# Batch 0's first three query blocks take seven second channel products from sums kept in the score squares' buffers

## The chip, the cores and the metric

One Trainium2 chip, one core. The metric is the device time of one execution in microseconds (us); a kernel's time is the median of its runs.

## The reference

Eight batches of a gated attention unit, followed by a mixer layer. With S = 3008, D = 256:

```
scores = z z^T / S                     (z: 3008 x 64, so scores are symmetric)
attn   = relu(scores)^2 @ v
x      = u * attn
h      = relu(x^T @ w_tok1) @ w_tok2   (token mixing, 256 wide)
u2     = x + h^T
out    = u2 + relu(u2 @ w_ch1) @ w_ch2 (channel mixing, 1536 wide)
```

## The kernel before, in words

A batch is cut into NQ = 6 query blocks of 512 rows (the last has 448) and, in the same places, into NG = 6 key groups of four 128-row tiles. A program of the host writes out the order of all instructions by hand: it keeps a modelled clock for TensorE (PE), ScalarE (ACT), VectorE (DVE) and the queue of SP, and at each step picks a unit of scores, half a group of attention (av), or a piece of the mixer. Its modelled times decide the order in which instructions are issued; on the chip, each engine works through its own list and waits only for data and buffers.

**Attention.** For block (b, q) and group g, two score units are made (L465), each of two 128 x 512 tiles, followed by a relu on ScalarE (L503; L491 for the half blocks on the diagonal, called triangles) and a square on VectorE (L511, L542). The squares lie in buffers of the tag `at`, of which there are six, 4 KB in each partition. As the scores are symmetric, a block's squares are also transposed by a DMA on SP's queue (`flip`, L562) into a buffer of the tag `fl` (eleven, also of 4 KB) and serve block (b, g) there; so in batch 1, block (1, q) scores only the groups g >= q, and (1, 3) scores three. Then v is multiplied in (L692), and two halves of the sum are added and gated by u (L820, L826, L846). `can_score` lets scores run ahead of the attention as long as `at` has room, and in batch 1 as far as one query block ahead.

**Mixing.** The mixer of batch b runs inside the attention of batch b + 1, in two stretches, in which no scores and no attention are issued: `goals` opens batch 0's token products at block (1, 2), its second token product and the channel mixing of its query blocks 0 to 2 (HALF = 3) at (1, 3), and the rest, with the first three blocks of batch 1, at (2, 0). Pieces of the mixer are:

- `tok1` (L1029) and `tok2` (L1086), with the addition of h to x on VectorE (L1095), and a transpose of u2 on SP (L1114);
- `ch1` (L1143): one of six parts of a query block's first channel product, four 128 x 512 matmuls into a pair of PSUM banks, evacuated with a relu to `h2pre` by ScalarE (L1182) or VectorE (L1184); the rule `on_act` chooses the engine from the modelled loads, and VectorE's limit is 1 us later for b > 0 than for batch 0;
- `ch2` (L1366): the second channel product by 128-row tiles, 12 matmuls of 128 x 256 for each of a block's four tiles, and `residual` (L1383), which adds u2 and sends the rows out;
- `product` (L1280): the second channel product in another form, used where `fast(q)` holds. The 2 x 2 blocks of (row tiles, channel tiles) are multiplied with seven products and not eight, in the manner of Strassen and Winograd. Each of the seven has 2 x 6 matmuls of 128 x 128 (half as many for the last query block). They take four sums of the hidden layer's tiles (`make_sums`, L1223, L1228, L1232, L1235, three times in a block, each into one `hsum` buffer), and sums of the weights (`mix_weights`, L989, made once). Each product is collected on VectorE with an addition into `ro` (L1317), and after the seventh `ro` is sent out. Product 5 waits for the addition of product 2, 6 for 1, 3 for 5, 7 for 6, 4 for 7, as they share banks.

In the kernel before, `fast(q)` holds for every query block but batch 0's first three and the very last one. `hsum` and `ro` lie in `fl`.

Around the second channel product of block q, parts of the first product of block q + 1 are issued early ("borrowed"): two in the ch2 form, five between the seven products. The sums of a borrowed query block 3 are put off (`late_sums`) to the last query block of the attention.

Of the kernel before, what the change touches and what calls it, by code (L numbers as in the profile page):

```python
# [57 lines left out]
def kernel(  # L58
# [914 lines left out]
    def mix_weights(t):  # L973
# [19 lines left out]

        step(t)

    VERY_LAST = (B - 1, NQ - 1, CHT // 2 - 1)
    ORDER_LAST = (1, 2, 6, 5, 0, 7, 3, 0, 4)

    def add_mixer(b):
# [130 lines left out]
        def ch1(q, c2, borrowed, end):  # L1130
            slots = [take_slot()[0] for _ in range(1 + ((b, q, c2) == VERY_LAST))]
            W = widths[q]
            xT = xTs[b, q]
            if c2 % 2 == 0:
                live["h2"] += 1
                st["h2", q, c2 // 2] = sb.tile(
                    [P, 4, QW], BF16, tag="h2", name="h2pre", bufs=ROOM["h2"])
            hps = [bank_pair(slot, "hp") for slot in slots]
            hp = hps[0]
            for r in range(2):  # L1140
                cc = 2 * c2 + r
                for dc in range(DT):
                    nc.tensor.matmul(  # L1143
                        hps[r % len(hps)][:, r, :W], w_ch1_sb[:, dc, cc * P:(cc + 1) * P],
                        xT[:, dc, :W], start=(dc == 0), stop=(dc == DT - 1))
            h2 = st["h2", q, c2 // 2][:, 2 * (c2 % 2):2 * (c2 % 2) + 2, :]

            def load(e):
                return max(free[e], end) + sum(op.busy for op in waiting[e])

            def keep_ends():
                if c2 == 0 and b % 2 == 0:
                    pair["hs"] = sb.tile([P, CHT, P], BF16, tag="hs", name="hs", bufs=1)
                r = b % 2 * TAIL
                copier = nc.gpsimd if b < B - 1 else nc.vector
                copier.tensor_copy(  # L1156
                    pair["hs"][:, 2 * c2:2 * c2 + 2, r:r + TAIL], h2[:, :, W - TAIL:W])

            if (b, q, c2) == VERY_LAST:
                landed, freed = [], Done()  # L1160

                def evacuate_part(r, t):
                    if r:
                        nc.scalar.activation(h2[:, r, :W], hps[1][:, r, :W], ACT.Relu)
                    else:
                        nc.vector.tensor_single_scalar(h2[:, r, :W], hp[:, r, :W], 0.0, AX.max)
                    landed.append(t)
                    if len(landed) == 2:
                        h2_done[q, c2].t = freed.t = max(landed)
                        keep_ends()  # L1170

                for r, engine, at, busy in ((0, "dve", end - 0.18, 0.62), (1, "act", end + 0.21, 0.5)):
                    push(engine, at, busy, busy + 0.16, lambda t, r=r: evacuate_part(r, t))
                ring.extend((freed, slot) for slot in slots)
                release("xT", xT_uses[q])
                return
            on_act = load("act") + 0.92 < load("dve") + 1.15 + (b > 0)

            def evacuate(t):
                recent[0] = h2[:, 0, :1]  # L1180
                if on_act:
                    nc.scalar.activation(h2[:, :, :W], hp[:, :, :W], ACT.Relu)  # L1182
                else:
                    nc.vector.tensor_single_scalar(h2[:, :, :W], hp[:, :, :W], 0.0, AX.max)  # L1184
                if q == NQ - 1:
                    keep_ends()
                if fast(q) and c2 % 2:
                    if borrowed and q == HALF and b < B - 1:
                        late_sums.append(lambda t: make_sums(q, c2 // 2, t))
                    else:  # L1190
                        make_sums(q, c2 // 2, t)
            engine, busy = ("act", 0.92) if on_act else ("dve", 1.15)
            ring.append((push(engine, end + 0.21, busy, busy + 0.16, evacuate,
                              done=h2_done[q, c2]), slots[0]))
            if c2 == CHT // 2 - 1:
                release("xT", xT_uses[q])
# [11 lines left out]
        def make_sums(q, d, t):  # L1208


            n = pairs_of(q)
            busy = 0.34 if n == 2 else 0.21
            sums = {}

            def kind(k):
                return sums["s"][:, k, :, :n, :]

            def add1(t):
                sums["s"] = sb.tile([P, 4, 2, 2, P], BF16, tag="fl", name="hsum", bufs=ROOM["fl"])
                st["sum", q, d] = sums["s"]  # L1220
                live["fl"] += 1
                fl_free.pop(0)
                nc.vector.tensor_add(kind(0), tiles_of(q, d, 0, 1), tiles_of(q, d, 1, 1))  # L1223
                push("dve", t - 0.05, busy, busy + 0.15, add3, done=s_done[q, d, 2])
                push("dve", t, busy, busy + 0.15, add2, done=s_done[q, d, 1])

            def add2(t):
                nc.vector.tensor_sub(kind(1), kind(0), tiles_of(q, d, 0, 0))  # L1228
                push("dve", t, busy, busy + 0.15, add4, done=s_done[q, d, 3])

            def add3(t):
                nc.vector.tensor_sub(kind(2), tiles_of(q, d, 0, 0), tiles_of(q, d, 0, 1))  # L1232

            def add4(t):
                nc.vector.tensor_sub(kind(3), tiles_of(q, d, 1, 0), kind(1))  # L1235

            push("dve", t, busy, busy + 0.15, add1, room=("fl",), frees=fl_free,
                 done=s_done[q, d, 0])

        h2_uses = [1] * NQ  # L1240
# [13 lines left out]
        def product(q, k, end):  # L1254
# [30 lines left out]
                done_with_h2(q)  # L1285
            if k == 7:
                for d in range(CHT // 4):
                    release("fl", [1], end + 0.2)
            collect(q, k, end)

        def collect(q, k, end):
# [17 lines left out]

            def add(t):  # L1310
                if k == 1:
                    st["res", q] = sb.tile([P, QW // P, D], F32, tag="fl", name="ro",
                                           bufs=ROOM["fl"])
                    live["fl"] += 1
                    fl_free.pop(0)
                m, h = blocks_of[k]
                nc.vector.tensor_add(  # L1317
                    res(m, h), source, us(m, h) if opening else res(m, h))
                recent[0] = st["res", q][:, 0, :1]
                over[q] -= 1  # L1320
                if not over[q]:
                    nc.sync.dma_start(
                        out=rows_of(out[b], q)[:, :2 * n, :], in_=st["res", q][:, :2 * n, :])
                    free["sp"] = max(free["sp"], t) + 0.4
                    release("fl", [1], t + 4.0)
                    release("us", us_uses[q])

            ready = end + 0.21
            done = taken[q, k]
            if k == 1:  # L1330
                with_u(q, ready, lambda at: push(
                    "dve", at, busy, busy + 0.15, add, first=1, room=("fl",), frees=fl_free,
                    done=done))
            else:
                done = push("dve", ready, busy, busy + 0.15, add, first=1, done=taken[q, k],
                            room=lambda: ("res", q) in st)
# [9 lines left out]

        def fast(q):

            return (b > 0 or q >= HALF) and (b, q) != (B - 1, NQ - 1)

        def ch2(q, half, i, end):
            apart = alone(q, half)
# [116 lines left out]
        for q in range(NQ):  # L1469
            while added[q] < CHT // 2:  # L1470
                add_next(q, q)
            rest = [(half, i) for half in halves(q) for i in range(pieces_of(q, half))]
            if fast(q):
                us_uses[q][0] += bool(rest)
                h2_uses[q] += bool(rest)
                for k in ORDER_LAST if q == NQ - 1 else (0, 0, 1, 2, 0, 6, 5, 0, 7, 3, 0, 4):
                    if k:
                        add_product(q, k)
                    elif rest:
                        add_ch2(q, *rest.pop(0))  # L1480
                    else:
                        add_next(q + 1, q)
            else:
                for _ in range(2):
                    add_next(q + 1, q)
                for half, i in rest:
                    add_ch2(q, half, i)
# [201 lines left out]
    def ask_w_tok1(c):  # L1689
        load_w_tok1(c)  # L1690
        if c == NG - 1:
            push("dve", pe[0] + 24.0, 0.28, 0.42, token_sums, first=-1)

    at_group(NQ * NG + HALF * NG + 2,
             lambda: push("dve", pe[0], 0.36, 0.5, mix_weights, first=-1))

    def ask_w_tok2(c):
# [39 lines left out]
    done_units = 2  # L1737
    NOW = 0.05
    STARVED = 0.7
    BACKLOG = 0.9  # L1740
    GRAIN = 2
    SPACING = 4.0
    while cur[0] is not None or heads or tails:
# [19 lines left out]
        if n and blk is not None and blk.b == 1:  # L1763
            b, q, _ = units[done_units][0]
            if b * NQ + q > NQ + blk.q + 1:
                n = 0
        slots = sorted(d.t for d, _ in ring if d.t is not None)
        n_now = min(n, len(slots))
        ts = FAR
# [115 lines left out]
```

## Time and profile before

| | us |
|---|---|
| median of 3 runs | 1116.48 |
| lowest, highest | 1116.16, 1121.13 |
| the profiled execution | 1116.06 |
| its span in the profile | 1114.0 |
| TensorE busy | 1108.1 (99%) |
| VectorE busy | 780.5 (70%) |
| ScalarE busy | 655.1 (59%) |
| GpSimd busy | 162.7 (15%) |

The profile is of one execution. A row of a timeline gives the start, the duration, the engine, the line (L1280 is line 1280 of the kernel), the operation, the tensors (out<-in), the shape and the count of merged instructions; square brackets hold the engine's idle time before the row and what ended it. A row of a group gives the count, the busy time, the mean duration in ns, and the idle time before. PE is TensorE's matmul, PEld its weight load, SPq and POOLq are instruction queues that issue DMAs. Matmuls are pipelined, so the rows of two neighbouring groups overlap by the time that the last matmul takes to drain.

### The profile page before, as it was taken

What the parts mean: (1) busy time and instruction counts of PE and PEld (TensorE: products, weight loads), DVE (VectorE), ACT (ScalarE), POOL (GpSimd) and SP (SyncE); (2) the same over time, 40 slices, a digit from 0 to 9 for tenths busy, and PEclk for the clock granted to TensorE, in tenths of its full rate; (3) what the DMA queues carried; (4) which work ended last, traced back from release to release, by engine and by line L of the source; (5) the groups of instructions that cost most, each with busy time, mean ns of one, the idle gap of its engine ahead of it and who ended that gap; (6) DMA issues with size and microseconds to landing.
All of it is one profiled execution on the core that took longest, in us unless ns stands there. A gap on an engine that the chain in (4) does not pass through costs nothing.

```text
span 1114.0 us, 26933 instructions
## 1 busy us (share of the span) xinstructions
PE 1108.1 (99%) x10965; PEld 675.6 (61%) x10965; DVE 780.5 (70%) x1855; ACT 655.1 (59%) x817; POOL 162.7 (15%) x382
## 2 busy tenths in 40 slices
PE   9999999999999999999999999999999999999998
PEld 3444574666557665576555865557655576556676
DVE  6889846875758757588566885578756787557775
ACT  8999524645854458545675356653666536743354
POOL 5321100211003110031000311003200120000000
PEclk9999999999999999999999999999999999999999
DMA  9999955796987979779597897868968678585213
GB/s 178 173 183 157 208 117 114 124 179 135 183 137 142 187 126 185 142 141 209 128 174 132 143 197 144 168 121 158 191 156 172 109 157 174 128 160 99 63 58 95
DMA packets 466155, 165.51 MB, mean 149 GB/s; under 512 B 433072, under 2 KB 449008, under 8 KB 466032
## 3 DMA queue, kind: packets, MB, share of 16 engines
q1 hardware_dynamic: 436640, 131.11, 58.0%
q0 software_dynamic: 28880, 32.32, 20.6%
q8 instruction: 85, 1.39, 0.5%
q10 hardware_dynamic: 512, 0.38, 0.1%
q14 instruction: 38, 0.31, 0.1%
HBM read 65.40 MB, written 24.64 MB: 81 GB/s over the span
## 4 chain that ended last, share of the span: by engine, by line
PE 97%; DVE 1%; ACT 1%; issue 1%; POOL 0%; DVEq 0%; POOLq 0%; ACTq 0%
PE acc L692 41%; PE hp L1143 21%; PE xb L1280 10%; PE zb L1280 7%; PE sc L465 6%; PE h_ps L1086 4%; PE a_ps L1029 3%; PE op L1366 3%; PE first_acc L609 1%; DVE a_f L1045 0%; ACT h2pre L1182 0%; PE wp L205 0%; ACT at L503 0%; POOL hs L1156 0%; DVE at L511 0%
## 5 line engine op out<-in xcount | busy, mean ns | idle before, releaser
L1182 ACT ACTIVATE h2pre<-hp 128x1024 bf16<-128x1024 f32 (+1 forms) x277 | 269.4, 1007 | 257.8 <-PE hp L1143 165.3
L692 PEld LDWEIGHTS <-v_sb 64*128 64x128 bf16 x4418 | 238.0, 94 | 219.3
L692 PE MATMUL acc<-at,v_sb 64*128 64x512 bf16 (+1 forms) x2738 | 338.8, 374 | 0.0
L503 ACT ACTIVATE at<-sc 128x1024 bf16<-128x1024 f32 (+1 forms) x290 | 287.5, 1027 | 72.2 <-PE sc L465 65.4
L511 DVE TENSOR_TENSOR at<-at 128x1024 bf16<-128x1024 bf16 (+1 forms) x290 | 198.5, 687 | 110.7 <-ACT at L503 106.7
L1143 PE MATMUL hp<-xT,w_ch_sb 128*128 128x512 bf16 (+1 forms) x1152 | 273.5, 375 | 0.1
L692 PE MATMUL acc<-fl,v_sb 64*128 64x512 bf16 (+1 forms) x1680 | 191.4, 367 | 0.0
L1143 PEld LDWEIGHTS <-w_ch_sb 128*128 128x128 bf16 x1152 | 106.2, 98 | 99.8 <-issue 3.0
L465 PE MATMUL sc<-zT 64*128 64x512 bf16 (+1 forms) x732 | 131.3, 360 | 0.1
L1280 PEld LDWEIGHTS <-hsum 128*128 128x128 bf16 x1944 | 115.9, 98 | 17.6 <-issue 1.1
L1280 PEld LDWEIGHTS <-h2pre 128*128 128x128 bf16 x1458 | 89.1, 98 | 19.3 <-issue 1.2
L820 ACT COPY cp<-acc 128x512 f32<-128x512 f32 (+1 forms) x94 | 54.9, 584 | 71.4 <-PE acc L692 59.8
L826 DVE TENSOR_TENSOR cp<-acc,cp 128x512 f32<-128x512 f32 (+1 forms) x94 | 63.5, 675 | 42.3 <-ACT cp L820 41.8
L491 ACT ACTIVATE at<-sc 128x512 bf16<-128x512 f32 (+3 forms) x152 | 56.1, 444 | 45.4 <-PE sc L465 45.0
L1223 DVE TENSOR_TENSOR hsum<-h2pre 128x512 bf16<-128x512 bf16 (+1 forms) x132 | 52.2, 400 | 37.7 <-ACT h2pre L1182 35.9
L1280 PE MATMUL xb<-w_mix_sb,hsum 128*128 128x128 bf16 x972 | 68.6, 219 | 0.4 <-DVE ro L1317 0.3
L542 DVE TENSOR_TENSOR at<-at 128x512 bf16<-128x512 bf16 (+3 forms) x152 | 41.5, 321 | 38.3 <-ACT at L491 38.2
L1317 DVE TENSOR_TENSOR ro<-xb,u_sb 128x256 f32<-128x256 f32 (+1 forms) x132 | 52.6, 399 | 21.9 <-PE xb L1280 20.2
L465 PEld LDWEIGHTS <-zT 64*128 64x128 bf16 x732 | 42.0, 94 | 41.8 <-issue 3.8
L124 POOL CAST mark<-at 128x1 f32<-128x1 bf16 x24 | 8.9, 369 | 375.2 <-DVE at L511 375.2
L846 DVE TENSOR_TENSOR xT<-cp,uT 128x512 bf16<-128x512 f32 (+1 forms) x94 | 62.4, 664 | 0.8
L1095 DVE TENSOR_TENSOR xT<-xT,h_ps 128x1024 bf16<-128x1024 bf16 (+1 forms) x48 | 54.6, 1172 | 4.7 <-PE h_ps L1086 4.6
(89 smaller groups left out, 983.0 us busy)
## 6 DMA issues: line engine op xcount, KB each, us to landing
out_dram<-ro SPq DMA_DIRECT2D x37, 512.0 KB, 2.9
v_sb<-in_v_dram POOLq DMA_DIRECT2D x40, 256.0 KB, 4.6
ur<-in_u_dram POOLq DMA_DIRECT2D x40, 256.0 KB, 5.1
w_tok_sb<-in_moe_w_tok_dram POOLq DMA_DIRECT2D x10, 256.0 KB, 10.7
zs<-in_z_dram POOLq DMA_DIRECT2D x35, 64.0 KB, 3.7
at<-at SPq DMA_TRANSPOSE x114, 2.4
out_dram<-ro SPq DMA_DIRECT2D x7, 256.0 KB, 2.2
fl<-at SPq DMA_TRANSPOSE x105, 4.4
```

The source lines that it names most:

```text
L465: nc.tensor.matmul(sc[:, r, c0:c1], zT[h, k:k + P], zT[h, m + c0:m + c1], start=True, stop=True)
L491: nc.scalar.activation(a3[:, i, c0:c1], sc[:, r, c0:c1], ACT.Relu, scale=inv_S)
L503: nc.scalar.activation(view, sv, ACT.Relu, scale=inv_S)
L511: nc.vector.tensor_mul(view, view, view)
L692: nc.tensor.matmul(o, vs[blk.b, g][rows, i, dh * P:(dh + 1) * P], rhs, start=(dh, h) not in blk.begun, stop=stop, skip_group_check=True)
L820: nc.scalar.copy(cp[:, :W], acc[:, 1, :W])
L826: nc.vector.tensor_add(cp[:, :W], acc[:, 0, :W], cp[:, :W])
L846: nc.vector.tensor_mul(xT[:, dh, :full * P].rearrange("p (t s) -> p t s", s=P), acc[:, :full * P].rearrange("p (t s) -> p t s", s=P), uT[: ...
L1095: nc.vector.tensor_add(to, to, h[:, :, :n * P].rearrange("p h (s t) -> p h t s", t=n))
L1143: nc.tensor.matmul(hps[r % len(hps)][:, r, :W], w_ch1_sb[:, dc, cc * P:(cc + 1) * P], xT[:, dc, :W], start=(dc == 0), stop=(dc == DT - 1))
L1182: nc.scalar.activation(h2[:, :, :W], hp[:, :, :W], ACT.Relu)
L1280: nc.tensor.matmul(to[:, i * P:(i + 1) * P], lhs, weights[:, c2, :], start=(first_use and c2 == 0 and i == 0), stop=(c2 == CHT // 2 - 1), ...
```

## The change

- `fast(q)` now holds for batch 0's query blocks 0, 1 and 2 as well, so they take seven products and their sums.
- Their `hsum` and `ro` buffers are taken from `at` (`home_of`, `take_home`, `frees_of`), not from `fl`.
- Query block 2 of batch 0 borrows three parts of query block 3's first product (`BORROW`) where the ch2 form borrowed two.
- While block (1, 2) is in its attention, at most one group of block (1, 3) is scored ahead (`AHEAD`).
- `mix_weights` is issued one query block earlier.
- `on_act` uses for batch 0 the limit that the other batches have.

```diff
+    BORROW = 3
...
-            on_act = load("act") + 0.92 < load("dve") + 1.15 + (b > 0)
+            on_act = load("act") + 0.92 < load("dve") + 2.15
...
             def add1(t):
-                sums["s"] = sb.tile([P, 4, 2, 2, P], BF16, tag="fl", name="hsum", bufs=ROOM["fl"])
+                home, n_home = take_home(q)
+                sums["s"] = sb.tile([P, 4, 2, 2, P], BF16, tag=home, name="hsum", bufs=n_home)
                 st["sum", q, d] = sums["s"]
-                live["fl"] += 1
-                fl_free.pop(0)
...
-            push("dve", t, busy, busy + 0.15, add1, room=("fl",), frees=fl_free,
+            push("dve", t, busy, busy + 0.15, add1, room=(home_of(q),), frees=frees_of(q),
                  done=s_done[q, d, 0])
...
             if k == 7:
                 for d in range(CHT // 4):
-                    release("fl", [1], end + 0.2)
+                    release(home_of(q), [1], end + 0.2)
...
                 if k == 1:
-                    st["res", q] = sb.tile([P, QW // P, D], F32, tag="fl", name="ro",
-                                           bufs=ROOM["fl"])
-                    live["fl"] += 1
-                    fl_free.pop(0)
+                    home, n_home = take_home(q)
+                    st["res", q] = sb.tile([P, QW // P, D], F32, tag=home, name="ro",
+                                           bufs=n_home)
...
-                    release("fl", [1], t + 4.0)
+                    release(home_of(q), [1], t + 4.0)
                     release("us", us_uses[q])
...
         def fast(q):
 
-            return (b > 0 or q >= HALF) and (b, q) != (B - 1, NQ - 1)
+            return (b, q) != (B - 1, NQ - 1)
+
+        def home_of(q):
+
+            return "fl" if b or q >= HALF else "at"
+
+        def take_home(q):
+
+            home = home_of(q)
+            live[home] += 1
+            frees_of(q).pop(0)
+            return home, ROOM[home]
+
+        def frees_of(q):
+
+            return {"fl": fl_free, "at": at_free}[home_of(q)]
...
                         add_ch2(q, *rest.pop(0))
-                    else:
+                    elif b or q != HALF - 1 or added[q + 1] < BORROW:
                         add_next(q + 1, q)
...
-    at_group(NQ * NG + HALF * NG + 2,
+    at_group(NQ * NG + (HALF - 1) * NG + 2,
              lambda: push("dve", pe[0], 0.36, 0.5, mix_weights, first=-1))
...
+    AHEAD = 1
...
             if b * NQ + q > NQ + blk.q + 1:
                 n = 0
+            if (b, q, blk.q) == (1, HALF, HALF - 1):
+                n = min(n, sum(u[0][:2] == (b, q) for u in units[:done_units]) < 2 * AHEAD)
```

More of the change, by code (lines that the diff above doesn't have):

```diff
@@ L1331, in collect @@
                 with_u(q, ready, lambda at: push(
-                    "dve", at, busy, busy + 0.15, add, first=1, room=("fl",), frees=fl_free,
-                    done=done))
+                    "dve", at, busy, busy + 0.15, add, first=1, room=(home_of(q),),
+                    frees=frees_of(q), done=done))
             else:
```

## The prediction

> **What bounds the kernel now.** The page comes first: its busy times and its chain.
>
> ```profile
> span 1114.0 us, 26933 instructions
> PE 1108.1 (99%) x10965; PEld 675.6 (61%) x10965; DVE 780.5 (70%) x1855; ACT 655.1 (59%) x817; POOL 162.7 (15%) x382
> PE acc L692 41%; PE hp L1143 21%; PE xb L1280 10%; PE zb L1280 7%; PE sc L465 6%; PE h_ps L1086 4%; PE a_ps L1029 3%; PE op L1366 3%; PE first_acc L609 1%; DVE a_f L1045 0%; ACT h2pre L1182 0%; PE wp L205 0%; ACT at L503 0%; POOL hs L1156 0%; DVE at L511 0%
> ```
>
> PE is busy in all but 1114.0 - 1108.1 = 5.9 us. So only two things can move the time: matmul time, and new gaps in PE. The profiled execution took 1116.06 us, 2.06 more than its span; the median of the three runs, 1116.48, is 0.42 above it. What a measurement of this kernel can tell from no change is about 0.5%, 5.6 us.
>
> Second view: PE's timeline where batch 0's first three query blocks are mixed.
>
> ```profile
> 127.79 3.63 PE L1086 MATMUL h_ps<-w_tok_sb,a_sb 128*128 128x512 bf16 x16
> ...
> 134.60 5.34 PE L1143 MATMUL hp<-xT,w_ch_sb 128*128 128x512 bf16 x24
> 139.78 5.40 PE L1366 MATMUL op<-w_ch_sb,h2pre 128*128 128x256 bf16 x48
> 145.02 5.34 PE L1143 MATMUL hp<-xT,w_ch_sb 128*128 128x512 bf16 x24
> 150.20 5.40 PE L1366 MATMUL op<-w_ch_sb,h2pre 128*128 128x256 bf16 x48
> 155.44 5.34 PE L1143 MATMUL hp<-xT,w_ch_sb 128*128 128x512 bf16 x24
> 160.62 5.40 PE L1366 MATMUL op<-w_ch_sb,h2pre 128*128 128x256 bf16 x48
> 165.96 0.45 PE L465 MATMUL sc<-zT 64*128 64x512 bf16 x4
> ```
>
> A row's length holds the drain of its last matmul, so durations are taken from start to start. A block takes 155.44 - 145.02 = 10.42 us, of which the second channel product (op) is 155.44 - 150.20 = 5.24, 109 ns for each of 48 matmuls. Nothing lies between the rows: this stretch, 38.2 us long, is pure matmul time.
>
> Third view: the same stage of batch 1, which already takes seven products.
>
> ```profile
> 249.58 2.75 PE L1143 MATMUL hp<-xT,w_ch_sb 128*128 128x512 bf16 x12
> 252.17 0.83 PE L1280 MATMUL xb<-w_ch_sb,h2pre 128*128 128x128 bf16 x12
> 252.84 0.83 PE L1280 MATMUL zb<-w_ch_sb,h2pre 128*128 128x128 bf16 x12
> 253.51 1.03 PE L1143 MATMUL hp<-xT,w_ch_sb 128*128 128x512 bf16 x4
> 254.38 0.83 PE L1280 MATMUL xb<-w_mix_sb,hsum 128*128 128x128 bf16 x12
> ...
> 258.78 0.83 PE L1280 MATMUL xb<-w_mix_sb,h2pre 128*128 128x128 bf16 x12
> 259.45 2.75 PE L1143 MATMUL hp<-xT,w_ch_sb 128*128 128x512 bf16 x12
> ```
>
> A block there takes 259.45 - 249.58 = 9.87 us: 24 first-product matmuls as before, and seven products of 12 matmuls at 252.84 - 252.17 = 0.67 us, 4.69 in all.
>
> Fourth view: the busy time of each engine by stretch (length, then PE, PEld, DVE, ACT, POOL, the granted clock, DMA).
>
> ```profile
> 115.16:127.79 12.63, 12.63 (x119) 5.57 (x117) 9.68 (x18) 11.53 (x12) 1.97 (x6) 1.00 1.19 199
> 127.79:165.96 38.17, 38.17 (x252) 24.19 (x250) 23.27 (x25) 11.84 (x12) 4.05 (x11) 1.00 0.73 152
> ...
> 165.96:187.23 21.27, 21.27 (x202) 10.22 (x202) 11.18 (x30) 6.45 (x13) 1.52 (x4) 1.00 0.58 116
> 187.23:204.13 16.90, 16.77 (x144) 8.24 (x141) 15.80 (x39) 15.92 (x22) 1.80 (x5) 1.00 0.45 76
> 249.58:259.45 9.87, 9.87 (x111) 7.04 (x109) 7.10 (x20) 6.01 (x7) 2.61 (x6) 1.00 1.07 184
> ```
>
> The granted clock is 1.00 throughout. ScalarE is nearly full before the mixing (11.53 of 12.63) and again at 187 to 204 (15.92 of 16.90), and nearly empty between (6.45 of 21.27). That pattern decides the rivals.
>
> **The change part by part.** *The products.* Three blocks lose 48 matmuls of 109 ns (5.24) and gain 84 that take 4.69: 3 x 0.55 = **1.65 us less PE time**. Start to start says the same: 10.42 - 9.87 = 0.55.
>
> A rule speaks against this. In twelve matmuls at 0.67 us, each with its own weight load, the spacing here is 56 ns. The Trainium skill, "TensorE: Matmul & The Clock Gate", section "Back-to-back issue gap", says that a stream of weight load and matmul pairs sustains about 81 ns a matmul at 128 columns, more than the isolated gap of some 56. By the skill's figure, 84 matmuls would be an estimated 6.80 us, 1.56 more than op, and the sum +4.7 instead of -1.65. The trace disagrees: 1.00 of the clock and 56 ns hold through whole blocks.
>
> *VectorE and ScalarE during the mixing.*
>
> ```profile
> L1184 DVE TENSOR_SCALAR h2pre<-hp 128x1024 bf16<-128x1024 f32 (+1 forms) x10 | 12.1, 1210 | 4.6 <-PE hp L1143 4.6
> L1383 DVE TENSOR_TENSOR res<-op,u_sb 128x512 f32<-128x512 f32 x6 | 4.2, 692 | 11.6 <-DMA out_dram<-res 7.6 <-PE op L1366 4.0
> L1223 DVE TENSOR_TENSOR hsum<-h2pre 128x512 bf16<-128x512 bf16 (+1 forms) x132 | 52.2, 400 | 37.7 <-ACT h2pre L1182 35.9 <-POOL hs L1156 1.4
> L1317 DVE TENSOR_TENSOR ro<-xb,u_sb 128x256 f32<-128x256 f32 (+1 forms) x132 | 52.6, 399 | 21.9 <-PE xb L1280 20.2
> ...
> PE xb L1280 <- DVE ro L1317: 1.0, 6, 0.2
> ```
>
> DVE gains 12 sums and 7 additions of results a block, 57 x 0.40 = 22.8 us. It loses six residuals (6 x 0.69 = 4.2) and, by the new rule for evacuations, most of its nine evacuations in the stretch (up to 9 x 1.21 = 10.9, which ScalarE takes over). So 23.3 + 22.8 - 4.2 - 10.9 = 31 of 37.4 us: full, but not over. Batch 1's block needs 7.10 of 9.87 and PE does not wait in it. Of all waits of PE for these additions the list shows six, 0.2 us at most. In the third block only three first-product parts of query block 3 may stand between the products, so its last four products follow each other; each waits for the addition behind the one before last, some 0.5 us (0.40 and its signals) against a product of 0.67. I take 0, and as bounds 0 to 0.5 us a block, nearest to the rows of batch 1; below 0 is excluded, as there is no gap here to close.
>
> *The moved part.* One more part of query block 3's first product (4 matmuls, 254.38 - 253.51 = 0.87 us) is done before 166 and not after 198. On PE that is neutral; it takes an evacuation of about 1 us out of the full stretch at 187 to 204, where PE shows a gap of 0.13. I take 0, with -0.2 as the bound.
>
> *The moved scores.* Block (1, 2) may now score one of block (1, 3)'s three groups ahead, not all three.
>
> ```profile
> 166.39 1.42 ACT L491 ACTIVATE at<-sc 128x512 bf16<-128x512 f32 x4 [5.33 <-PE sc L465]
> 167.67 1.98 ACT L503 ACTIVATE at<-sc 128x1024 bf16<-128x1024 f32 x2
> ...
> 189.44 7.64 ACT L503 ACTIVATE at<-sc 128x1024 bf16<-128x1024 f32 x8
> ...
> 200.46 5.62 ACT L1182 ACTIVATE h2pre<-hp 128x1024 bf16<-128x1024 f32 x6
> ```
>
> L491 is the triangle of (1, 4), the first relu after the mixing: all of (1, 3) was scored before it. Four units move behind the mixing, each with score matmuls (neutral on PE), a relu of 7.64 / 8 = 0.96 to 1.03 us and a square.
>
> ```profile
> L503 ACT ACTIVATE at<-sc 128x1024 bf16<-128x1024 f32 (+1 forms) x290 | 287.5, 1027 | 72.2 <-PE sc L465 65.4
> L511 DVE TENSOR_TENSOR at<-at 128x1024 bf16<-128x1024 bf16 (+1 forms) x290 | 198.5, 687 | 110.7 <-ACT at L503 106.7
> 182.05 5.34 PE L692 MATMUL acc<-fl,v_sb 64*128 64x512 bf16 x48
> 120.71 14.02 SPq L562 DMA_TRANSPOSE fl<-at  x5
> ```
>
> Block (1, 3) restarts with one own group and its three flipped groups: four of six. A group takes PE 5.2 / 3 = 1.73 us, so 6.9 us of work covers 4 x 1.03 + 0.69 = 4.8 us of ScalarE and VectorE. Two transposes go with them: 14.02 / 5 = 2.8 us each on SP's queue, now ahead of those of (1, 4)'s triangle and of x. The first wanted is (1, 3, 4) in block (1, 4), one block (10.4 us) later. I take 0; the other end is that all four relus come back later: 4.1 us.
>
> *Buffers.* Six: one holds the score group, a block takes three sums and one result, and one is left for the next block's first sums. The rest of those follow the release behind the sixth product; 12 sums of 0.4 are 4.8 us, and 7 us of PE work lies before they are read (five parts of 0.87 and four products of 0.67). The result's buffer comes back with its transfer:
>
> ```profile
> out_dram<-ro SPq DMA_DIRECT2D x37, 512.0 KB, 2.9
> w_ch_sb<-in_moe_w_ch_dram POOLq DMA_DIRECT2D x4, 384.0 KB, 13.6
> 63.72 0.83 POOL L297 DMA_DIRECT2D w_ch_sb<-in_moe_w_ch_dram  x1 [0.81 <-DMA w_tok_sb<-in_moe_w_tok_dram]
> ```
>
> 2.9 us is under the 3.8 that pass until the block after next asks (three parts of 0.87 and an evacuation). A sum that waits stands in DVE's queue ahead of the additions of results and of squares; a wait of a few tenths stays under the cover above. *The mixed weights* come one block earlier, in block (1, 2), which begins at 115.16; their source landed by about 63.7 + 0.8 + 13.6 = 78. Eight short subtractions replace the four squares (4 x 0.69) that leave that stretch. Nothing.
>
> **The sum:** -1.65, with bounds -1.85 and about +4: 1116.06 - 1.65 = 1114.4 on the profiled execution, **1114.8 us** as a median (0.42 higher).
>
> **The rivals.** *The scores come back (slower).* The four relus fill ScalarE's idle time only if they run at once after the mixing. Should they, or their transposes, slip past 187, they join a stretch in which ScalarE has 1 us left, and the second mixing starts late by up to 4.1 us: 1114.8 + 4.1 = **1118.9**. For it: ScalarE and VectorE are 94% busy there. Against: ScalarE idles 21.27 - 6.45 = 14.8 us before, over three times the need. It decides when less than 4.1 us of that can be used.
>
> *VectorE takes it back.* If sums or additions come 0.5 us late in each block, 1.5 of 1.65 us is gone: **1116.3**, no change. For it: VectorE goes from 61 to 83% of the stretch and has one block's start (tok2's six additions) in front of its first sums. Against: batch 1 does the same with no gap. A change that in effect does nothing (the blocks mixed as before) would look the same here and is told apart by the op rows.
>
> *The weight loads bind.* A product's matmul streams half the columns of op's behind a weight load of the same size.
>
> ```profile
> L1280 PEld LDWEIGHTS <-hsum 128*128 128x128 bf16 x1944 | 115.9, 98 | 17.6 <-issue 1.1
> ```
>
> A load takes 98 ns: under op's 109 a matmul, over the products' 56. Were loads not to overlap, 84 of them would take 8.23 us a block, 2.99 more than op: 1116.48 + 9.0 = **1125.5**. Against: 56 ns is the spacing in every row of batch 1, so there they overlap; it decides from a spacing of 62 ns (5.24 / 84). The skill's section named above states a rule of this kind.
>
> **How the numbers follow.** Forecast 0.71 (its own range 1113.8 to 1115.8), VectorE takes it back 0.13, scores come back 0.11, weight loads 0.01, something not priced 0.04, nearly all of it slower. The first two make 0.84; the range reaches a little into the third and takes the spread of the runs: 1113.3 to 1118.0. Faster by over 0.5% would need more than PE's whole idle time or three times the saving: 0.01. Slower by over 0.5% takes a wait of over 7 us that no row shows: 0.04. Within 0.5%: 0.95.
>
> **What would show it.** Right: blocks of about 9.87 us from 145 on, op gone from there, the stretch from tok2 to the first score about 38.2 - 1.65 + 0.87 = 37.4 us, the second mixing one part shorter, and each stage behind it about 1.65 us earlier. The scores' rival would show as a PE gap near 170 or 200, VectorE's as waits of PE for ro or hsum between 140 and 165. Wrong: if the products are spaced over 62 ns, or if PE's idle time rises above 8 us.

## The result, and the profile after

The changed kernel takes 1113.42 us (median of 7 runs, 1113.05 to 1114.11) against 1117.12 for the kernel before (7 runs beside it, 1115.44 to 1121.13): a ratio of 0.9969, interval 0.9959 to 0.9979, that is -3.5 us (-4.6 to -2.3). Measured again on another occasion: 1113.48 (12 runs) against 1116.25 (31 runs), ratio 0.9966, interval 0.9953 to 0.9980. The profiled executions differ by 1113.31 - 1116.06 = -2.75. The kernel is faster, by less than 0.5%; the forecast was 1114.8, -1.65.

First the page of the changed kernel: busy times and chain.

```profile
span 1111.5 us, 27200 instructions
PE 1106.5 (100%) x11073; PEld 679.2 (61%) x11073; DVE 784.9 (71%) x1896; ACT 664.8 (60%) x827; POOL 163.0 (15%) x382
...
PE 99%; DVE 1%; issue 0%
```

The chain by engine in the kernel before:

```profile
PE 97%; DVE 1%; ACT 1%; issue 1%; POOL 0%; DVEq 0%; POOLq 0%; ACTq 0%
```

PE's busy time fell by 1108.1 - 1106.5 = 1.6 us, the three blocks' matmul time, and its idle time from 5.9 to 5.0. VectorE and ScalarE do more, and ScalarE is no longer on the chain. PE's timeline of the first mixing shows the blocks:

```profile
139.31 0.83 PE L1280 MATMUL xb<-w_ch_sb,h2pre 128*128 128x128 bf16 x12
...
146.59 2.75 PE L1144 MATMUL hp<-xT,w_ch_sb 128*128 128x512 bf16 x12
149.18 0.83 PE L1280 MATMUL xb<-w_ch_sb,h2pre 128*128 128x128 bf16 x12
149.84 0.83 PE L1280 MATMUL zb<-w_ch_sb,h2pre 128*128 128x128 bf16 x12
...
156.46 2.75 PE L1144 MATMUL hp<-xT,w_ch_sb 128*128 128x512 bf16 x12
...
163.94 0.83 PE L1280 MATMUL xb<-w_mix_sb,h2pre 128*128 128x128 bf16 x12
164.70 0.39 PE L465 MATMUL sc<-zT 64*128 64x512 bf16 x2
```

A block takes 156.46 - 146.59 = 9.87 us, as batch 1's do, and no row of the stretch has an idle time before it. The same stretches as before (length; PE, PEld, DVE, ACT, POOL; clock; DMA):

```profile
115.47:127.23 11.76, 11.76 (x111) 5.17 (x109) 9.91 (x23) 7.64 (x8) 2.19 (x6) 1.00 1.27 197
127.23:164.70 37.47, 37.47 (x362) 24.57 (x361) 29.09 (x66) 21.22 (x22) 4.31 (x10) 1.00 0.54 118
146.59:156.46 9.87, 9.87 (x112) 7.04 (x110) 6.97 (x20) 5.79 (x7) 1.77 (x4) 1.00 0.38 88
164.70:186.00 21.30, 21.30 (x203) 11.89 (x203) 9.37 (x20) 10.76 (x17) 1.53 (x4) 1.00 0.65 130
186.00:202.30 16.30, 16.30 (x147) 9.63 (x144) 14.91 (x33) 14.89 (x20) 1.80 (x5) 1.00 0.86 142
```

The first mixing is 37.47 us long (37.4 forecast), VectorE 78% busy in it. ScalarE was relieved ahead of the mixing (7.64 of 11.76, where it had 11.53 of 12.63) and does the moved relus after it, in time that was idle (10.76 of 21.30 where it had 6.45 of 21.27).

From such rows of PE's timeline comes the table on which all that follows rests: each stage of each kernel from start to start, in us. The columns are: where tok1 of batch 0 starts; from there to tok2 (the attention of block (1, 2) lies in it); the first mixing, to the first score behind it; the attention, to the start of the last attention matmul of (1, 5), which lies 0.28 before the second mixing's first row; the second mixing, to tok1 of batch 1; all that is behind it, to the last matmul; the sum from tok1.

| kernel | tok1 at | to tok2 | first mixing | attention | second mixing | rest | sum |
|---|---|---|---|---|---|---|---|
| before | 110.37 | 17.42 | 38.17 | 32.41 | 22.38 | 889.56 | 999.94 |
| all undone (e1) | 110.17 | 17.42 | 38.17 | 32.41 | 22.39 | 889.33 | 999.72 |
| changed | 110.67 | 16.56 | 37.48 | 33.30 | 21.22 | 888.96 | 997.52 |
| changed, again (e5) | 116.42 | 16.56 | 37.48 | 33.30 | 21.23 | 888.93 | 997.50 |
| one block (e2) | 110.40 | 16.56 | 38.94 | 33.31 | 21.23 | 889.26 | 999.30 |
| before, 3 borrowed (e3) | 114.37 | 17.42 | 39.39 | 32.41 | 21.74 | 890.05 | 1001.01 |
| before, new rule (e4) | 110.43 | 17.42 | 38.17 | 32.41 | 22.46 | 889.18 | 999.64 |
| before, 1 group ahead (e6) | 110.53 | 16.56 | 38.59 | 33.30 | 22.09 | 889.06 | 999.60 |
| changed, 2 borrowed (e7) | 110.41 | 16.56 | 36.75 | 33.30 | 22.09 | 888.93 | 997.63 |
| changed, old rule (e8) | 110.36 | 16.56 | 38.74 | 33.30 | 21.23 | 888.91 | 998.74 |
| changed, 0 ahead (e9) | 111.94 | 16.13 | 37.48 | 33.52 | 21.38 | 889.59 | 998.10 |
| changed, 2 ahead (e10) | 110.40 | 16.99 | 37.56 | 32.84 | 21.23 | 888.88 | 997.50 |
| before, no result marks (e11) | 110.52 | 17.42 | 38.38 | 32.41 | 22.39 | 889.42 | 1000.02 |

The sum is 2.2 to 2.4 us shorter than in the two profiles of the kernel before: -0.86 - 0.69 + 0.89 - 1.16 = -1.82 to tok1 of batch 1, and -0.4 to -0.6 behind it. Another 0.3 lies after the last matmul (span end less its start: 1111.54 - 1108.19 = 3.35 against 1113.96 - 1110.31 = 3.65).

### The profile page after: what moved, and what is told of

The parts are those of the page before. It is cut to its first block, busy times and chain, and to the rows that moved or that the text cites. A ratio compares the mean times of both kernels' runs of the same rounds, so it can differ in the third digit from the quotient of the medians.

```text
span 1111.5 us, 27200 instructions
## 1 busy us (share of the span) xinstructions
PE 1106.5 (100%) x11073; PEld 679.2 (61%) x11073; DVE 784.9 (71%) x1896; ACT 664.8 (60%) x827; POOL 163.0 (15%) x382
## 4 chain that ended last, share of the span: by engine, by line
PE 99%; DVE 1%; issue 0%
PE acc L692 42%; PE hp L1144 22%; PE xb L1280 11%; PE zb L1280 8%; PE sc L465 7%; PE h_ps L1087 4%; PE a_ps L1030 3%; PE op L1380 1%; PE first_acc L609 1%; DVE a_f L1046 0%; PE wp L205 0%; PE first_acc L205 0%; DVE a_f L1050 0%; DVE a_f L1058 0%; PE first_acc L184 0%; DVE ro L1316 0%
## 5 line engine op out<-in xcount | busy, mean ns | idle before, releaser
L1183 ACT ACTIVATE h2pre<-hp 128x1024 bf16<-128x1024 f32 (+1 forms) x287 | 278.5, 1008 | 249.6 <-PE hp L1144 163.9
L692 PEld LDWEIGHTS <-v_sb 64*128 64x128 bf16 x4418 | 241.6, 94 | 215.8
L1280 PEld LDWEIGHTS <-hsum 128*128 128x128 bf16 x2088 | 124.4, 98 | 18.2 <-issue 0.4
L1280 PEld LDWEIGHTS <-h2pre 128*128 128x128 bf16 x1566 | 95.6, 98 | 20.5 <-issue 1.2
L1223 DVE TENSOR_TENSOR hsum<-h2pre 128x512 bf16<-128x512 bf16 (+1 forms) x141 | 55.9, 400 | 40.3 <-ACT h2pre L1183 39.5
L1280 PE MATMUL xb<-w_mix_sb,hsum 128*128 128x128 bf16 x1044 | 73.6, 219 | 0.0
L1316 DVE TENSOR_TENSOR ro<-xb,u_sb 128x256 f32<-128x256 f32 (+1 forms) x141 | 56.2, 399 | 23.0 <-PE xb L1280 20.9
```

The source lines that it names most:

```text
L692: nc.tensor.matmul(o, vs[blk.b, g][rows, i, dh * P:(dh + 1) * P], rhs, start=(dh, h) not in blk.begun, stop=stop, skip_group_check=True)
L1280: nc.tensor.matmul(to[:, i * P:(i + 1) * P], lhs, weights[:, c2, :], start=(first_use and c2 == 0 and i == 0), stop=(c2 == CHT // 2 - 1), ...
L1316: nc.vector.tensor_add(res(m, h), source, us(m, h) if opening else res(m, h))
```

## The experiments

As the medians said -3.5 and the sum of the forecast -1.65, four theories stood against each other. **A**: the matmul time, and small waits that the profiles show. **B**: the stretch at 187 to 204, full on ScalarE and VectorE, costs more in an ordinary run than in the one profiled, and the borrowed part relieves it. **C**: the rule for evacuations. **D**: something that the profiles do not show.

**e1, everything undone** (against the changed kernel).

```diff
+            return (b > 0 or q >= HALF) and (b, q) != (B - 1, NQ - 1)
...
+            on_act = load("act") + 0.92 < load("dve") + 1.15 + (b > 0)
...
+    at_group(NQ * NG + HALF * NG + 2,
...
+    AHEAD = 3
```

> Every part of the change undone in the changed source: the instructions are those of the kernel before, engine by engine. All theories: 0.0 us against the kernel before; its spread shows how far two sets of runs of one program lie apart, and its profile is a second one of the kernel before. Theory A (the matmul time alone): the gap of PE near 201 us is again 0.1 to 0.2. Theory B (the full stretch of ScalarE and VectorE at 187 to 204 us costs more in an ordinary run than in the one profiled): the gap there differs from the first profile's, up to 2 us.

1116.21 us (11 runs) against 1116.47 (35 runs), ratio 1.0001 (0.9993 to 1.0010). The second profile agrees with the first in every stage up to tok1 of batch 1, the gap of 0.14 at 201 included; B finds nothing here. "Rest" differs by 0.23 between two profiles of one program: differences of that size in it are not read below.

**e2, products in one block only.**

```diff
-            return (b, q) != (B - 1, NQ - 1)
+            return (b > 0 or q >= 2) and (b, q) != (B - 1, NQ - 1)
```

> Only query block 2 of batch 0 takes seven products; blocks 0 and 1 keep the 128 x 256 form. Three parts are still borrowed, and one score group is ahead. Theory A (matmul time, 0.55 us a block, and about 0.2 for the moved part): -0.75 us against the kernel before. Theory B (the relieved stretch at 187 to 204): -0.55 and the rest of the change's excess, -2.0 to -2.5. Theory C (the rule for evacuations): -2.0 to -2.5 as well.

1115.39 against 1116.47, ratio 0.9988 (0.9977 to 1.0000): -1.3 us with an interval from -2.6 to 0. Theories B and C wanted -2.0 to -2.5, which the interval does not exclude; the stages do. To tok1 of batch 1 the sum is 0.35 shorter than before, the full change's 1.82. The first mixing is that of e6 (below), 38.59, plus the third part (0.87) and less one block's 0.55: 38.91, measured 38.94; both hold one wait of PE behind a residual. So the saving goes by blocks.

**e3, the third borrowed part alone.**

```diff
-                for _ in range(2):
+                for _ in range(3 if (b, q) == (0, HALF - 1) else 2):
                     add_next(q + 1, q)
```

> The kernel before, except that its query block 2 borrows three parts of block 3's first product and not two. Theory A: -0.2 us (the one gap of PE). Theory B: -1.5 to -2.0, with less spread between its runs. Theory C: 0.

1116.75 against 1116.47, ratio 1.0006 (0.9998 to 1.0015). The first mixing grows by 1.22, more than the part's 0.87, since PE waits once behind a residual (0.20 us in its list of waits), and the second shrinks by 0.65, less than that; the gap of 0.14 is still in it. B falls, and theory A's -0.2 did not come either.

**e4, the rule for evacuations alone.**

```diff
-            on_act = load("act") + 0.92 < load("dve") + 1.15 + (b > 0)
+            on_act = load("act") + 0.92 < load("dve") + 2.15
```

> The kernel before with the new rule for evacuations alone: ten of batch 0's evacuations go from VectorE to ScalarE. Theory A: 0.0 us. Theory B: 0.0, or slower by up to 1, as ScalarE is the fuller engine in the stretch at 187 to 204. Theory C: -1.5 to -2.0.

1116.26 against 1116.47, ratio 0.9998 (0.9989 to 1.0007), the first mixing 38.17 as before. C falls as a source of gain.

**e5, the change again.**

> The changed kernel as it is, on the same chip and beside the same runs of the kernel before as the next three. From the profiles of before and after, start to start on PE: the first mixing -0.70 us, the attention of blocks 1,2 to 1,5 together +0.05, the second mixing -1.17, the later batches -0.43: -2.25. Theory A (this sum is the whole effect; what medians show beyond it is chance of the first 20 us): -2.0 to -2.5 us. Theory D (something that the profiles do not show gives another 1 us): -3.0 to -3.5.

Ratio 0.9966 (0.9953 to 0.9980); medians 1113.48 - 1116.25 = -2.8, the lowest runs 1112.91 - 1115.37 = -2.5. The sum in its profile, 997.50, is the first one's to 0.02. By the stages -2.2 to -2.4, with the 0.3 behind the last matmul -2.5 to -2.7: that is within both intervals and beside the medians, so A may be enough. D is not ruled out: the two ratios stand for -3.5 and -3.8 us, and the runs of the changed kernel and its variants with three such blocks spread less. Of these, 2 of 50 lie over 1.5 us above the lowest of their set, of the kernel before 34 of 90 (of e1, with the same instructions, 2 of 11). No profile shows why, so about 1 us stays open. This profile shows one source of the spread, since its execution took 1119.04 us. Its wait of PE (us in all, times, longest) and its first stretches:

```profile
PE sc L465 <- DMA zT<-zr: 4.0, 1, 4.0
...
9.00:13.00 4.00, 0.52 (x4) 0.03 (x1) 2.12 (x4) 0.77 (x1) 3.23 (x6) 0.88 1.42 178
13.00:17.00 4.00, 3.46 (x14) 1.19 (x14) 0.84 (x2) 1.94 (x2) 1.06 (x2) 0.50 1.50 179
17.00:21.00 4.00, 3.67 (x17) 1.25 (x17) 2.31 (x4) 2.56 (x3) 2.65 (x5) 0.76 1.22 200
```

A transpose of batch 0's z came 4.0 us late, PE stood still, and the clock granted behind that was 0.50 over 4 us and 0.76 over the next 4: tok1 starts at 116.42 and not near 110.4. All that follows takes the same time. The profile of e3, with tok1 at 114.37, has the same wait with 2.0 us.

**e6, fewer scores ahead, alone.**

```diff
-    AHEAD = 3
+    AHEAD = 1
```

(against e1)

> The kernel before, except that block 1,2 scores at most one group of block 1,3 ahead. Theory A with the score order as the cause of the shorter second mixing: attention before the first mixing -0.87 us, after it +0.90, second mixing 22.1 and not 22.4 us: -0.3 in all. If the score order is not that cause: second mixing 22.4, 0.0 in all. The rival of the prediction (the scores come back): second mixing up to 4.1 us later.

1116.62 against 1116.25, ratio 0.9998 (0.9988 to 1.0008). The stages divide it: -0.86 to tok2, +0.89 in the attention behind the mixing (the four moved units), -0.30 in the second mixing, as the theory of the score order had it; but +0.42 in the first mixing, so nothing is left. Most of that is one wait in a first channel product, behind a residual: two matmuls start at 146.78 and 147.33, 0.55 apart and not 0.22. The view gives this loss of 0.34 as 0.17 of idle time, because a row counts as busy until its last matmul has drained: in the rows above, 12 matmuls last 0.83 us and the next row starts after 0.67. So the idle time shown is 0.16 short of what a wait costs. The second mixing has the same trap. Its first rows on PE, before:

```profile
198.65 5.65 PE L1143 MATMUL hp<-xT,w_ch_sb 128*128 128x512 bf16 x24
204.13 0.83 PE L1280 MATMUL xb<-w_ch_sb,h2pre 128*128 128x128 bf16 x12
```

and in the changed kernel:

```profile
198.29 4.49 PE L1144 MATMUL hp<-xT,w_ch_sb 128*128 128x512 bf16 x20
202.62 0.83 PE L1280 MATMUL xb<-w_ch_sb,h2pre 128*128 128x128 bf16 x12
```

Before, 24 matmuls take 204.13 - 198.65 = 5.48 us where 24 of 0.216 are 5.18; in the changed kernel 20 take 4.33, which is 20 of 0.216. So the wait of 0.14 at 201 costs 0.30, all that the second mixing of e6 gains. Why it is gone, ScalarE's timeline shows, first before:

```profile
200.03 0.53 ACT L820 COPY cp<-acc 128x448 f32<-128x448 f32 x1 [0.69 <-DVE xT L851]
200.46 2.86 ACT L1182 ACTIVATE h2pre<-hp 128x1024 bf16<-128x1024 f32 x3
```

then in the changed kernel:

```profile
199.24 0.53 ACT L820 COPY cp<-acc 128x448 f32<-128x448 f32 x1 [0.25 <-DVE xT L851]
199.66 4.70 ACT L1183 ACTIVATE h2pre<-hp 128x1024 bf16<-128x1024 f32 x5
```

The first evacuation of the second mixing waits behind a copy of the attention's result, and that copy waits for VectorE's gating: 0.69 us before, 0.25 after (and in e6). The mixing itself starts at 198.65 and 198.29, so the first evacuation comes 1.81 and 1.37 us into it, and PE, which waited for a bank at 201, does not any more.

**e7, two parts borrowed.**

```diff
-    BORROW = 3
+    BORROW = 2
```

> The changed kernel with two parts of query block 3's first product borrowed, not three. Theory A: first mixing 36.6 us, second mixing +0.87 and up to 0.3 of waits: 0.0 to 0.3 slower than the change, so -2.0 us against before. Theory D-borrow (the third part buys the excess): 1 us slower than the change.

Ratio 0.9964 (0.9951 to 0.9976), the change's own; sum 997.63 against 997.50. The first mixing is 0.73 shorter, the second 0.87 longer. The third part is worth 0.1 us: the relief of the second mixing comes from the score order, not from this part.

**e8, the old rule for evacuations.**

```diff
-            on_act = load("act") + 0.92 < load("dve") + 2.15
+            on_act = load("act") + 0.92 < load("dve") + 1.15 + (b > 0)
```

> The changed kernel with the old rule for batch 0's evacuations, so VectorE takes four more of them, 1.2 us each, while it makes the sums. Prediction: VectorE at 83% of the first mixing goes to 95%, and a wait of PE of up to 1 us appears there: 0 to 1 us slower than the change. Theory A (PE alone counts): the same as the change, first mixing 37.5 us.

1114.68 against the change's 1113.48 beside it, ratio to before 0.9981 (0.9971 to 0.9991): 1.2 us of the saving is gone. The whole of it is in the first mixing, 38.74 and not 37.48. VectorE, PE and the stretch:

```profile
136.62 1.22 DVE L1185 TENSOR_SCALAR h2pre<-hp 128x1024 bf16<-128x1024 f32 x1
...
139.09 1.21 DVE L1185 TENSOR_SCALAR h2pre<-hp 128x1024 bf16<-128x1024 f32 x1
...
142.42 0.42 DVE L1228 TENSOR_TENSOR hsum<-hsum,h2pre 128x512 bf16<-128x512 bf16 x1
```

```profile
142.90 0.40 PE L1280 MATMUL xb<-w_mix_sb,hsum 128*128 128x128 bf16 x4 [1.09 <-DVE hsum L1228]
```

```profile
126.92:165.66 38.74, 37.34 (x357) 24.59 (x362) 33.00 (x70) 18.00 (x18) 4.11 (x10) 1.00 0.56 116
```

Two evacuations stand among the first block's sums, the last sum is ready at 142.84, and product 6 waits 1.09 us for it, which with the 0.16 of drain is the whole loss. This is the prediction's rival "VectorE takes it back", in its place and by its mechanism, at 33.00 / 38.74 = 85% of VectorE (95% was expected). The new rule, worth nothing by itself (e4), is what keeps it away.

**e9, none ahead.**

```diff
-    AHEAD = 1
+    AHEAD = 0
```

> The changed kernel with no group of block 1,3 scored before the mixing: six score units behind it, and the block restarts with three flipped groups alone. The prediction's account of the cover: six relus and a square are 6 x 1.03 + 0.69 = 6.9 us, against 3 x 1.73 of attention and 6 x 0.22 of scores = 6.5 us on PE; so a gap of about 0.4 us (0 to 1) near 170, else as the change. The rival (the scores come back in the full stretch at 187 to 204): the second mixing 1 to 2 us later.

Ratio 0.9969 (0.9957 to 0.9981), as the change. The forecast gap of 0.4 us near 170 is not there; PE's timeline passes from the flipped groups to the first own one without a wait:

```profile
168.79 0.38 PE L465 MATMUL sc<-zT 64*128 64x512 bf16 x2
169.01 1.03 PE L692 MATMUL acc<-fl,v_sb 64*128 64x512 bf16 x8
169.87 0.38 PE L465 MATMUL sc<-zT 64*128 64x512 bf16 x2
170.09 1.03 PE L692 MATMUL acc<-at,v_sb 64*128 64x512 bf16 x8
```

My account let the attention wait for all six relus. It needs the first group's two, and the next ones come while that group is multiplied: ScalarE's six relus run from 165.98 to 172.40. The second mixing is 0.16 longer than in the change, far from the rival's 1 to 2. "Rest" is 0.6 longer in this profile; 0.35 of it is one wait of PE for an addition to `ro`, at 899 us, and the cause of the remainder stays open.

**e10, two groups ahead.**

```diff
-    AHEAD = 1
+    AHEAD = 2
```

> The changed kernel with two groups of block 1,3 scored ahead: four score buffers are left to the mixing, which takes four in a block. If buffers are the limit, the first sums of the next block wait for the sixth product's release, under the 7 us of cover: 0.0; with the cover gone, a wait of up to 1 us in the second and third block. If the score order is what shortens the second mixing, that is 22.4 - 0.87 = 21.5 and not 21.2 us: 0.3 slower than the change.

1113.22 (5 runs), ratio 0.9969 (0.9957 to 0.9981), sum 997.50. With four buffers left the first mixing takes 37.56 where five give 37.48, so buffers do not bind. The second mixing stays at 21.23 (0.3 more was expected if it went by the count of groups). So the extra 0.30 is seen only where all three groups are ahead, as in the kernel before.

**e11, no pacing copies of results**, on the kernel before.

```diff
-                recent[0] = st["res", q][:, 0, :1]
+                pass
```

> The kernel before, except that GpSimd's pacing copies never read a result buffer (they read the last score or hidden buffer). That takes 17 waits of VectorE's sums for GpSimd away; the order of PE, VectorE, ScalarE and SP is untouched. If such a wait is what the later batches of the kernel before lose against the change: token product to token product, the fourth interval 135.8 us and not 136.1, the fifth 136.7: -0.35 us. If not: 0.0, and the fourth interval stays at 136.1.

In "rest", one interval differs steadily, the fourth: from tok1 of batch 3 to that of batch 4 it is 136.09 and 136.12 us in the two profiles of the kernel before, 135.93 to 136.35 in its variants without products in the first blocks (e3, e4, e6, e11), and 135.76 or 135.77 in every kernel with them. There the first sum of a last query block waits, and PE then waits for an addition, here in the kernel before:

```profile
626.57 0.83 PE L1280 MATMUL xb<-w_mix_sb,hsum 128*128 128x128 bf16 x12 [0.16 <-DVE ro L1317]
```

With the drain that is the interval's 0.32. For the first sum, the list of VectorE's waits names GpSimd before, and in e11, without those copies of GpSimd's, the transfer that sends a result out:

```profile
DVE hsum L1223 <- POOL hs L1156: 1.4, 2, 0.7
```

```profile
DVE hsum L1223 <- DMA out_dram<-ro: 1.4, 2, 0.9
```

The interval is 136.31 in e11, and the ratio 0.9992 (0.9977 to 1.0008): no gain. My theory of GpSimd's copies falls. By the second list the sum's buffer was a result's buffer that was still being sent out. That the changed kernel hands its buffers round in another order, and so misses this, is only argued.

## Why the prediction was right

**The products: -1.65, measured so.** A block is 9.87 us, PE's busy time fell by 1.6. The first mixing is 37.48 against 38.17 - 1.65 + 0.87 = 37.39; the 0.09 lies in tok2, whose first 12 matmuls take 129.92 - 127.23 = 2.69 us and not 12 x 0.216 = 2.59. The spacing of 56 ns holds here too (149.84 - 149.18 over 12 matmuls). The Trainium skill, "TensorE: Matmul & The Clock Gate", section "Back-to-back issue gap", has 81 ns for such a stream; the rows disagree, and "the weight loads bind" fell with them.

**VectorE: no wait, but nearer to the edge than I said.** I counted 83% and 0 to 0.5 us a block; it is 78% and 0. e8 shows the edge: at 85% one block lost 1.25 us (1.09 by the view), more than the 0.5 I allowed a block. The rows of batch 1 were the right ones to lean on, and the new rule a real part of the forecast.

**The moved part: 0, and it is 0.1 (e7).** I put the relief of the second mixing here, with -0.2 as its bound.

**The moved scores: the step that was mis-sized.** I took 0 with +4.1 as the other end. They cost nothing, not even with none ahead (e9), so the rival "the scores come back" fell. And they gave something: -0.30 in the second mixing (e6 and e7: 22.09 against 22.39). I had excluded a gain of this size, as only PE's 0.13 of idle time in the stretch at 187 to 204 seemed to be there to take, and gave the moved part -0.2 as a bound. That was the misreading: from start to start the same wait is 0.30. The chain of waits of the kernel before, in order of time, shows what I did not use:

```profile
189.44 2.98 ACT at L503 x3
192.41 0.02 issue
192.44 0.69 DVE at L511
...
200.46 1.04 ACT h2pre L1182
201.50 0.04 issue
201.54 2.75 PE hp L1143 x12
```

From 189 to 201 it runs through ScalarE and VectorE, and it ends at the matmul that waited. So their order of work set when PE went on, and another order could close the wait without any matmul being saved. In e6 alone the gain is undone by the wait behind a residual in the first mixing; no row of the change's first mixing has such a wait.

**What the sum left out.** -0.4 to -0.6 in the later batches and -0.3 behind the last matmul. The first is waits of PE for an addition to `ro` in a last query block, 0.3 us each from start to start: the one at 626 us that e11 looks at, and another at 764 in the first profile of the kernel before alone. Neither profile of the changed kernel has one, but e2 and e9 have one at 899. The second lies in the end of the program, and was luck, since no term foresaw it. The last transfer lands 2.43 us after the start of the last matmul before and 2.44 after. SP then goes through waits for the semaphores of transfers, one every 0.06 us: six are left before and one after (seven in e2, whose end is another 0.06 longer). Why the last transfer's semaphore has another place in that list is not shown. Together with the 0.30 and what the first mixing took back, they carry -1.65 to about -2.6, which is 1113.9 from 1116.48. The measured 1113.42 is below that and below the forecast's own range (1113.8 to 1115.8), and only 0.12 inside the range given (1113.3 to 1118.0). That it lies inside is in part luck: its main term was right, but about 1 us of the effect was in no term of the sum, and about as much again, between the stages and the ratio, no profile shows.

No kernel tried beats the changed one: e7, e9 and e10 have its ratio within 0.0005. The earlier place of the mixed weights was not tried apart.

## What to carry to other kernels

Where PE is full and a later stage already runs the new form, take its price from that stage, from start to start: 0.55 us a block was right to the hundredth. Then ask which engine pays for the saved matmuls, and look at the one block in which it also has other work: one rule for evacuations, worth nothing alone, kept 1.2 us of the gain (e8). And where the chain of waits leaves the full engine for a stretch, leave room for a gain there when the change moves work in or out of the stretch or before it, and size that room from start to start: the wait shown as 0.14 was worth 0.30.

## What the runs showed of the hardware that I had not expected

A pause of 4.0 us at the start cost 6 us in all, by a clock of 0.50 over 4 us and 0.76 over another 4 (e5). The Trainium skill, "TensorE: Matmul & The Clock Gate", section "What's actually happening", tells of a gate that halves the clock after an idle window of some 3.4 us; the trace of e5 agrees, with 0.50 behind 4.0 us. In e3, though, a pause of 2.0 us was enough: the granted clock behind it was 0.50 from 14.5 to 17 us. Executions of one program that differ by 5.7 us (1113.31 and 1119.04) agree to 0.02 us in the 997.5 us behind tok1 (the two profiles of the kernel before to 0.22 in 999.9), so stages compared from start to start resolve tenths where medians of a dozen runs leave an interval of 3 us.
